# Alternating dK products with o, dQ and dV products on TensorE, and giving VectorE both gradient products in one unit of eight

## The chip, the cores and the metric

One core of a Trainium2 chip; the batches of runs fell on different chips, so each had its own runs of the kernel before beside it. The time is device microseconds (us) of one execution; lower is better. Each program ran several times.

Names: TensorE (PE in the profile, its weight loads PEld) does matrix products into PSUM, the memory that products land in, cut into banks that tiles use in turn. VectorE (DVE), ScalarE (ACT) and GpSimd (POOL) do elementwise work; taking a result out of PSUM is called an eviction. SP issues DMAs.

Tiles in the profile: `sps` scores in PSUM, `eT` their exponentials, `eN` the same transposed by DMA; `dps` the gradient product in PSUM, `cp` its copy, `dsT` the gradient of the scores, `dsx` its transpose; `oq` the PSUM bank of o and dQ, `oTs` the copy of o out of it; `qX` the queries that dK needs. Names in `R` are long-lived buffers.

## The reference, cut to what matters

The program is the forward pass and all gradients of two attention blocks. Block A, linear attention, runs first and is not touched. The change sits in block B: attention of 16 query heads over one shared key and value head, sequence 2048, head width 28.

```python
scores = jnp.einsum("bhqd,bkd->bhqk", q, k) * (Dh ** -0.5)
p = _softmax(scores, axis=-1)
o = jnp.einsum("bhqk,bkd->bhqd", p, v)
# and its gradients (jax.vjp): dV = p^T do, dS = p * (do v^T - rowsum), dQ = dS k, dK = dS^T q
```

## The kernel before

Block B is one software-pipelined loop of 512 *units* (plus a tail). Eight units make a *block*: two heads, 256 queries, all 2048 keys, 256 keys a unit. In unit `u` the kernel starts the scores of unit `u`, the gradient product for the scores of unit `w = u - 16`, and consumes older results. Two banks of PSUM (`psD`, two buffers, two tiles a unit) hold the gradient product, three hold scores.

```python
for u in range(NU + 28):
    w = u - 16
    # ... two score tiles sp, two gradient tiles dp
    rows_SD(u, sp, dp)                       # TensorE: scores of u, dP of w
    if hasS:                                 # ScalarE
        nc.scalar.activation(out=et[:, u % 2, 0, :], in_=sp[0][:, :], func=ACT.Exp, scale=scale)
    if hasD:
        nc.vector.tensor_tensor(out=dst[:, 0, :], in0=dp[0][:, :], in1=ew[:, w % 2, 0, :], op=ALU.mult)
        cp = pc_.tile([P, 512], BF16, name="cp")
        nc.scalar.activation(out=cp[:, :], in_=dp[1][:, :], func=ACT.Copy)
        nc.gpsimd.tensor_tensor(out=dst[:, 1, :], in0=cp[:, :], in1=ew[:, w % 2, 1, :], op=ALU.mult)
    if hasS:
        nc.scalar.activation(out=et[:, u % 2, 1, :], in_=sp[1][:, :], func=ACT.Exp, scale=scale)
    # ... once a block: transposes of o (unit 1) and of do (unit 6), small products
    x = u - 28                               # dK: 16 groups of 4 products a block, in units 4 to 7, 0, 1
    # ...
    v = u - 1
    y = u - 18                               # o of the unit before, dQ of the dsT two units old
    for t2 in range(2):
        # o:  vaug x eT of v        dQ:  kn x dsT[y]
    if u >= 18 and u % 8 in (2, 3):          # dV, half of it in each of two units
        # ...
    if 0 <= v < NU and v % 8 == 7:           # unit 0: VectorE takes o out of PSUM (oTs)
        nc.vector.tensor_copy(out=oTs[v // 8][:, :], in_=oq[0:64, 0:256])
    if 0 <= y < NU and y % 8 == 7:           # unit 1: ScalarE takes dQ out of PSUM
        nc.scalar.activation(out=qT_B[g][...], in_=oq[64:128, 0:256], func=ACT.Copy, scale=scale)
    # VectorE: 32x32 transposes of dsT[u - 18] into dsx, for dK
```

So `dsT`, the gradient of the scores, has two halves: VectorE makes one straight from PSUM. The other is copied by ScalarE (`cp`) and multiplied by GpSimd, because GpSimd cannot read PSUM (the Trainium skill, "Trainium Kernel Development and Optimization", Key Constraints).

Of the kernel before, what the change touches and what calls it, by code (L numbers as in the profile page):

```python
# [8 lines left out]
ACT = mybir.ActivationFunctionType  # L9
ALU = mybir.AluOpType  # L10
AX = mybir.AxisListType
BF16 = mybir.dt.bfloat16
# [5 lines left out]
P = 128  # L18
# [6 lines left out]
def kernel(  # L25
# [21 lines left out]
    nc = tc.nc  # L47
# [518 lines left out]
    NB = 64  # L566
    NU = NB * 8
# [3 lines left out]
    with ExitStack() as cs_:  # L571
# [8 lines left out]
        pc_ = cs_.enter_context(tc.tile_pool(name="ccp", bufs=3, side="right"))  # L580
# [7 lines left out]
        eT, eN, dsT, dsx, qX, onat, don, doT, rl, oTs, prod = ({} for _ in range(11))  # L588

        def mmt(out, lhsT, rhs, pos, start, stop):  # L590
            nc.tensor.matmul(out, lhsT=lhsT, rhs=rhs, start=start, stop=stop, tile_position=pos,  # L591
                             skip_group_check=True)

        def blk(b):
            qc, pair = divmod(b, 8)
            return qc, pair, pair // 2, pair % 2
# [91 lines left out]
        with tc.manual_schedule():  # L688
            for u in range(NU + 28):
                w = u - 16  # L690
# [12 lines left out]
                dp = [psD.tile([P, 512], F32, name="dps") for _ in range(2)] if hasD else None  # L703
# [7 lines left out]
                if hasD:  # L711
                    dst = pd_.tile([P, 2, 512], BF16, name="dsT")
                    dsT[w] = dst
                    ew = eT[w // 2]
                    nc.vector.tensor_tensor(out=dst[:, 0, :], in0=dp[0][:, :], in1=ew[:, w % 2, 0, :], op=ALU.mult)  # L715
                    cp = pc_.tile([P, 512], BF16, name="cp")
                    nc.scalar.activation(out=cp[:, :], in_=dp[1][:, :], func=ACT.Copy)  # L717
                    nc.gpsimd.tensor_tensor(out=dst[:, 1, :], in0=cp[:, :], in1=ew[:, w % 2, 1, :], op=ALU.mult)  # L718
                if hasS:
                    nc.scalar.activation(out=et[:, u % 2, 1, :], in_=sp[1][:, :], func=ACT.Exp, scale=scale)  # L720
                    if u % 2 == 1:
# [5 lines left out]
                if e >= 0 and e % 8 == 0 and e // 8 < NB:  # L727
                    b = e // 8
# [6 lines left out]
                    if pair == 0:  # L735
# [9 lines left out]
                                            op=ALU.mult)  # L745
# [7 lines left out]
                if e >= 0 and e % 8 == 0 and e // 8 < NB:  # L753
                    b = e // 8
# [3 lines left out]
                        out=prod[b][:],  # L758
                        in0=do_nat[:, 2 * qc:2 * qc + 2, pair * 64:pair * 64 + 64].rearrange(
                            "p q (h c) -> p q h c", c=32),  # L760
                        in1=onat[qc][:, :, pair * 64:pair * 64 + 64].rearrange("p q (h c) -> p q h c", c=32),
                        op=ALU.mult)
                e = u - 12
                if e >= 0 and e % 8 == 0 and e // 8 < NB:
                    b = e // 8
# [4 lines left out]
                if e >= 0 and e % 8 == 0 and e // 8 < NB:  # L770
                    b = e // 8
# [7 lines left out]
                    doT[b] = pw_.tile([P, 256], BF16, name="doT")  # L779
                    nc.vector.tensor_copy(out=doT[b][r:r + 64, :], in_=tp2[r:r + 64, 0:256])  # L780

                x = u - 28
                if 0 <= x and x // 8 < NB and x % 8 < 6:
                    b = x // 8
                    qc, pair, g, hp = blk(b)
                    m0 = 3 * (x % 8) - max(0, x % 8 - 4)
                    for m in range(m0, m0 + (3 if x % 8 < 4 else 2)):
                        h, B, s = m // 8, (m // 2) % 4, m % 2
                        for a in range(4):
                            rhs = dsx[b][32 * a:32 * a + 32, :, h, :, :].rearrange(  # L790
                                "p u t (b i s) -> p u t b i s", b=4, s=2)[:, :, :, B, :, s]
                            mmt(dk_acc[32 * a:32 * a + 32, :],
                                qX[qc][32 * a:32 * a + 32, B, s, pair * 64 + 32 * h:pair * 64 + 32 * h + 32],
                                rhs, (32 * a, 32 * a), b == 0 and m == 0, b == NB - 1 and m == 15)

                v = u - 1
                y = u - 18
                for t2 in range(2):
                    if 0 <= v < NU:
                        b, tp = divmod(v, 8)  # L800
                        t = 2 * tp + t2
                        for h in range(2):
                            mmt(oq[32 * h:32 * h + 32, 0:256], vaug[:, t, :],
                                eT[v // 2][:, v % 2, h, t2 * 256:(t2 + 1) * 256], (0, 32 * h), t == 0, t == 15)
                    if 0 <= y < NU:
                        b, tp = divmod(y, 8)
                        t = 2 * tp + t2
                        for h in range(2):
                            mmt(oq[64 + 32 * h:96 + 32 * h, 0:256], kn[:, t, :],
                                dsT[y][:, h, t2 * 256:(t2 + 1) * 256], (0, 64 + 32 * h), t == 0, t == 15)  # L810
                if u >= 18 and u % 8 in (2, 3) and (u - 18) // 8 < NB:
                    b, h = divmod(u - 18, 8)
                    for qb in range(2):
                        for c in range(4):
                            rhs = eN[4 * b + c][:, :, :].rearrange("p (u h t q) k -> p u h t q k", u=2, h=2,
                                                                   t=2)[:, :, h, :, qb, :]
                            mmt(dv_acc[32 * c:32 * c + 32, :], don[b][:, qb, h, :], rhs, (0, 32 * c),
                                b == 0 and h + qb == 0, b == NB - 1 and h + qb == 2)
# [20 lines left out]
                if u % 64 in (16, 24) and u > 64:  # L839
                    out_proj(2 * (u // 64 - 1) + u % 64 // 8 - 2)  # L840

                if 0 <= v < NU and v % 8 == 7:
                    oTs[v // 8] = pm_.tile([64, 256], F32, name="oTs")
                    nc.vector.tensor_copy(out=oTs[v // 8][:, :], in_=oq[0:64, 0:256])  # L844
                if 0 <= y < NU and y % 8 == 7:
                    qc, pair, g, hp = blk(y // 8)
                    nc.scalar.activation(out=qT_B[g][64 * hp:64 * hp + 64, qc * 256:(qc + 1) * 256],
                                         in_=oq[64:128, 0:256], func=ACT.Copy, scale=scale)
                if 0 <= y < NU:
                    b, tp = divmod(y, 8)  # L850
                    if tp == 0:
                        dsx[b] = px_.tile([P, 8, 2, 2, 256], BF16, name="dsx")
                    nc.vector.transpose(  # L853
                        out=dsx[b][:, tp, :, :, :].rearrange("p h t c -> p (h t c)").bitcast(F32),
                        in_=dsT[y][:, :, :].rearrange("p h c -> p (h c)").bitcast(F32))
# [11 lines left out]
        for c in range(4):  # L867
            nc.vector.tensor_copy(out=dkvT[32:64, c * 512:(c + 1) * 512], in_=dv_acc[32 * c:32 * c + 32, :])
            nc.scalar.activation(out=dkvT[0:32, :].rearrange("p (t a i) -> p t a i", a=4, i=32)[:, :, c, :],
                                 in_=dk_acc[32 * c:32 * c + 32, :].rearrange("p (t i) -> p t i", i=32), func=ACT.Copy,  # L870
# [15 lines left out]
        for c in range(4):  # L886
            r = DC_ROWS[c]
            ps = gen(0)
            for st in range(NS):
# [3 lines left out]
                                 func=ACT.Copy)  # L893
# [44 lines left out]
```

## Time and profile before

| | before |
|---|---|
| median time | 1176 us (1173 to 1179) |
| units 16 to 511 of the loop | about 280 to 1090 us |
| a block with no output projection in it | 12.78 us |
| first exponential to first exponential, usual unit | 1.46 us |
| ScalarE start to start, 128x512 from PSUM | 0.49 us (duration 0.60) |
| GpSimd multiply, 128x512 | 1.15 us |

The table of stretches for the kernel before, 400 us in mid-loop. Columns: stretch, its length, then busy time and number of instructions of PE, PEld, DVE, ACT and POOL, the TensorE clock that was granted (1 is full), the DMA share (summed time of the packets over 16 engines, so it can pass 1), GB/s.

```profile
500.00:900.00 400.00, 383.22 (x6550) 142.05 (x6550) 357.16 (x655) 384.82 (x771) 310.71 (x339) 1.00 1.10 182
```

ScalarE is busy 96% and TensorE 96% of it, VectorE 89%, GpSimd 78%. TensorE's figure does not tell how near it is to its limit (the Trainium skill, "Perfetto Trace Analysis", section "Identifying the Most-Contended Engine", says so because matmuls are pipelined; E6 below comes back to it).

The timeline of ScalarE before, one block; columns are start, length, engine, line, operation, output and input, count and, in brackets, the idle time before. L710 is the first exponential of a unit, L847 the dQ eviction. The first line is unit 7 of the block ahead; then come units 0 to 7.

```profile
725.43 0.60 ACT L710 ACTIVATE eT<-sps 128x512 bf16<-128x512 f32 x1 [0.24 <-PE dps L591]
...
726.94 0.60 ACT L710 ACTIVATE eT<-sps 128x512 bf16<-128x512 f32 x1
...
728.39 0.61 ACT L710 ACTIVATE eT<-sps 128x512 bf16<-128x512 f32 x1
...
730.01 0.38 ACT L847 ACTIVATE R_63<-oq 64x256 bf16<-64x256 f32 x1
730.42 0.60 ACT L710 ACTIVATE eT<-sps 128x512 bf16<-128x512 f32 x1
...
731.88 0.61 ACT L710 ACTIVATE eT<-sps 128x512 bf16<-128x512 f32 x1
...
733.40 0.60 ACT L710 ACTIVATE eT<-sps 128x512 bf16<-128x512 f32 x1
...
734.85 0.61 ACT L710 ACTIVATE eT<-sps 128x512 bf16<-128x512 f32 x1
...
736.40 0.60 ACT L710 ACTIVATE eT<-sps 128x512 bf16<-128x512 f32 x1
...
738.21 0.60 ACT L710 ACTIVATE eT<-sps 128x512 bf16<-128x512 f32 x1 [0.24 <-PE dps L591]
```

Read the starts of L710: 1.45 to 1.55 us apart where ScalarE just runs through three evictions. The Trainium skill, page "ScalarE: Activation LUTs", section "What ACT_TABLE_LOAD costs", says that back-to-back ACTIVATEs overlap by about 93 ns; this trace comes near it (0.60 us long, 0.49 us apart, so 0.11 us). Only two units are longer: unit 1 with the eviction (2.03) and unit 6 (1.81). I use the distance from an odd unit to the next odd unit below, because the change works in pairs: 2.96, 3.49, 2.97 and 3.36 us into units 1, 3, 5 and 7.

The waits of the loop before (from 260 to 1090 us): engine, line, what it waited for, total us, times, longest.

```profile
POOL dsT L718 <- ACT cp L717: 155.1, 310, 7.7
...
ACT eT L710 <- PE dps L591: 28.3, 79, 2.9
```

GpSimd waits for ScalarE's copies (155 us; it has time to spare), and ScalarE's first exponential seldom waits for products (28 us). Nobody is seen waiting long for GpSimd. The group of the dQ matmuls on the page before says it too; its columns are line, engine, operation, tile names, shapes, count, then busy us and mean ns, then idle us just before and the part put down to one releaser:

```profile
L591 PE MATMUL oq<-dsT,R_65 128*32 128x256 bf16 x2048 | 203.1, 278 | 1.1 <-POOL dsT L718 0.9
```

The dQ matmuls stood 1.1 us in the whole run, 0.9 of it for GpSimd's multiply.

### The profile page before, as it was taken

The numbers are of one execution on the slowest core, as the hardware profiler recorded it, in microseconds if no ns is written. First come the engines' busy times: TensorE is split into PE (matmuls) and PEld (weight loads), VectorE is DVE, ScalarE is ACT, GpSimd is POOL, SyncE is SP. The second block draws the span as 40 slices with busy tenths as digits, with TensorE's granted clock in tenths as the row PEclk, the third lists the DMA queues.
The fourth block names the chain that finished last, engine by engine and source line by source line (L and its number), as shares of the span: only waits on it lengthen the run. The fifth ranks groups of instructions, "written<-read, shape, count | busy, mean of one in ns | idle before, by whom it ended". The sixth has DMA issues, their size and how long they took to land. (4 is left out here: it accounts for less than half of the span.)

```text
span 1172.0 us, 38434 instructions
## 1 busy us (share of the span) xinstructions
PE 1099.7 (94%) x15388; PEld 444.6 (38%) x15388; DVE 885.5 (76%) x1669; ACT 900.9 (77%) x1788; POOL 699.4 (60%) x835
## 2 busy tenths in 40 slices
PE   7999997988989999999999999999999999999998
PEld 4555543333333333333333333333333333333344
DVE  7886400336889898888889888988999899888922
ACT  3453112357989999999999999999999999999511
POOL 9000150003777777777778777877787778777900
PEclk9999998989999999999999999999999999999999
DMA  9779897059999999999999999999999999999962
GB/s 259 126 130 184 160 188 177 20 125 198 180 179 190 188 164 187 190 184 175 189 188 160 199 188 186 162 198 188 152 195 182 189 170 199 184 168 163 240 147 75
DMA packets 684435, 202.91 MB, mean 173 GB/s; under 512 B 651232, under 2 KB 679392, under 8 KB 684256
## 3 DMA queue, kind: packets, MB, share of 16 engines
q1 hardware_dynamic: 673664, 190.26, 94.8%
q10 hardware_dynamic: 9312, 6.65, 2.1%
q0 software_dynamic: 1280, 3.55, 1.1%
q8 instruction: 120, 1.97, 0.7%
q14 instruction: 59, 0.48, 0.1%
HBM read 22.83 MB, written 15.03 MB: 32 GB/s over the span
## 5 line engine op out<-in xcount | busy, mean ns | idle before, releaser
L718 POOL TENSOR_TENSOR dsT<-cp,eT 128x512 bf16<-128x512 bf16 x512 | 590.3, 1153 | 193.2 <-ACT cp L717 156.2
L715 DVE TENSOR_TENSOR dsT<-dps,eT 128x512 bf16<-128x512 f32 x512 | 347.8, 679 | 58.3 <-PE dps L591 37.6
L853 DVE STREAM_TRANSPOSE dsx<-dsT 128x512 f32<-128x512 f32 x512 | 357.8, 699 | 1.3 <-POOL dsT L718 0.3
L710 ACT ACTIVATE eT<-sps 128x512 bf16<-128x512 f32 x512 | 307.3, 600 | 42.2 <-PE dps L591 28.3
L591 PEld LDWEIGHTS <-R_65 32*128 32x128 bf16 (+1 forms) x8192 | 171.5, 92 | 403.3 <-issue 356.1
L717 ACT ACTIVATE cp<-dps 128x512 bf16<-128x512 f32 x512 | 305.1, 596 | 12.0 <-PE dps L591 11.1
L720 ACT ACTIVATE eT<-sps 128x512 bf16<-128x512 f32 x512 | 311.6, 609 | 0.0
L591 PE MATMUL dk_acc<-dsx,qX 32*32 32x512 bf16 x4096 | 290.4, 377 | 0.0
L591 PE MATMUL dps<-doT,R_65 32*128 32x256 bf16 x2048 | 253.9, 271 | 7.7 <-DVE R_64 L824 1.1
L591 PE MATMUL sps<-R_63,R_65 32*128 32x256 bf16 x2048 | 242.9, 276 | 5.9 <-ACT eT L710 2.0
L591 PE MATMUL oq<-eT,R_65 128*32 128x256 bf16 x2048 | 213.8, 278 | 2.5 <-issue 0.3
L591 PE MATMUL oq<-dsT,R_65 128*32 128x256 bf16 x2048 | 203.1, 278 | 1.1 <-POOL dsT L718 0.9
L591 PEld LDWEIGHTS <-qX 32*32 32x32 bf16 x4096 | 69.4, 89 | 94.1 <-issue 54.1
L591 PE MATMUL dv_acc<-eN,don 128*32 128x512 bf16 x1024 | 86.9, 382 | 2.5 <-DMA eN<-eT 2.5
L521 DVE TENSOR_TENSOR osb<-R_65 32x512 bf16<-32x512 bf16 x4 | 1.7, 413 | 74.2 <-ACT R_65 L518 74.2
L380 POOL MEMSET ga<- 64x448 bf16 x2 | 0.9, 468 | 90.8 <-PE agen L337 71.3
L553 POOL MEMSET R_65<- 128x16 bf16 x1 | 0.2, 172 | 70.8 <-DVE R_65 L552 70.8
L748 POOL TENSOR_TENSOR don<-R_64,rl 128x128 bf16<-128x128 bf16 x64 | 25.8, 403 | 21.4 <-DVE rl L740 21.4
L844 DVE COPY oTs<-oq 64x256 f32<-64x256 f32 x64 | 26.5, 414 | 15.1 <-PE oq L591 14.4
L731 PE MATMUL sps<-identF,oTs 64*128 64x64 f32 x128 | 21.3, 247 | 17.0 <-DVE oTs L844 10.6
L591 PEld LDWEIGHTS <-don 128*32 128x32 bf16 x1024 | 34.7, 97 | 4.0 <-issue 3.9
L79 PEld LDWEIGHTS <-R_64 128*128 128x128 bf16 x256 | 23.9, 100 | 28.0 <-issue 10.3
(216 smaller groups left out, 961.2 us busy)
## 6 DMA issues: line engine op xcount, KB each, us to landing
qX<-qn_d SPq DMA_DIRECT2D x128, 64.0 KB
out_dram<-osb ACTq DMA_DIRECT2D x44, 112.0 KB
eN<-eT SPq DMA_TRANSPOSE x256
qn_d<-dsx SPq DMA_DIRECT2D x1, 2048.0 KB
on_d<-onat SPq DMA_DIRECT2D x8, 256.0 KB
xa<-in_A_x_dram SPq DMA_DIRECT2D x8, 224.0 KB
ga<-in_grad_out_dram SPq DMA_DIRECT2D x4, 448.0 KB
xa<-in_grad_out_dram POOLq DMA_DIRECT2D x4, 448.0 KB, 4.7
```

Of the source, the lines that this page charges most:

```text
L79: nc.tensor.matmul(out_ap, lhsT=lhsT, rhs=rhs, start=start, stop=stop, tile_position=(0, 0))
L521: nc.vector.tensor_tensor(out=sq[0:32, :], in0=kT[0:32, qc * 512:(qc + 1) * 512], in1=kT[0:32, qc * 512:(qc + 1) * 512], op=ALU.mult)
L591: nc.tensor.matmul(out, lhsT=lhsT, rhs=rhs, start=start, stop=stop, tile_position=pos, skip_group_check=True)
L710: nc.scalar.activation(out=et[:, u % 2, 0, :], in_=sp[0][:, :], func=ACT.Exp, scale=scale)
L715: nc.vector.tensor_tensor(out=dst[:, 0, :], in0=dp[0][:, :], in1=ew[:, w % 2, 0, :], op=ALU.mult)
L717: nc.scalar.activation(out=cp[:, :], in_=dp[1][:, :], func=ACT.Copy)
L718: nc.gpsimd.tensor_tensor(out=dst[:, 1, :], in0=cp[:, :], in1=ew[:, w % 2, 1, :], op=ALU.mult)
L720: nc.scalar.activation(out=et[:, u % 2, 1, :], in_=sp[1][:, :], func=ACT.Exp, scale=scale)
L731: nc.tensor.transpose(onp[:, qb, :, :].rearrange("p h c -> p (h c)"), oTs[b][0:64, qb * P:(qb + 1) * P], identF[0:64, 0:64], tile_position ...
L748: nc.gpsimd.tensor_tensor(out=dn[:], in0=dnv, in1=r_[:].to_broadcast([P, 2, 2, 32]), op=ALU.mult)
L844: nc.vector.tensor_copy(out=oTs[v // 8][:, :], in_=oq[0:64, 0:256])
L853: nc.vector.transpose(out=dsx[b][:, tp, :, :, :].rearrange("p h t c -> p (h t c)").bitcast(F32), in_=dsT[y][:, :, :].rearrange("p h c -> p ...
```

## The change

Its intent: TensorE goes through fewer kinds of work per unit. Before, nearly every unit had scores, dK, then o and dQ. Now odd units have scores and dK (four groups of four at once), even units have scores and a double portion of o and dQ, with dV in two of them. And in unit 2 of a block VectorE makes both halves of dsT, which relieves ScalarE of one `cp` and GpSimd of one multiply.

```diff
-                    cp = pc_.tile([P, 512], BF16, name="cp")
-                    nc.scalar.activation(out=cp[:, :], in_=dp[1][:, :], func=ACT.Copy)
-                    nc.gpsimd.tensor_tensor(out=dst[:, 1, :], in0=cp[:, :], in1=ew[:, w % 2, 1, :], op=ALU.mult)
+                    if u % 8 == 2:
+                        nc.vector.tensor_tensor(out=dst[:, 1, :], in0=dp[1][:, :], in1=ew[:, w % 2, 1, :], op=ALU.mult)
+                    else:
+                        # cp and the GpSimd multiply as before
...
-                x = u - 28
-                if 0 <= x and x // 8 < NB and x % 8 < 6:
+                x = u - 27
+                if 0 <= x and x // 8 < NB and x % 2 == 0:
...
-                v = u - 1
-                y = u - 18
-                for t2 in range(2):
+                v, y = u - 1, u - 17
+                for d in range(4 if u % 2 == 0 else 0):
+                    t2 = d % 2
+                    v_, y_ = v - 1 + d // 2, y - 1 + d // 2
...                  # o of v_, dQ of dsT[y_]
-                if u >= 18 and u % 8 in (2, 3) and (u - 18) // 8 < NB:
+                if u >= 18 and u % 8 in (2, 4) and (u - 18) // 8 < NB:
...
-                if 0 <= v < NU and v % 8 == 7:          # oTs
+                if u % 2 == 0 and 0 <= v < NU and v % 8 == 7:
-                if 0 <= y < NU and y % 8 == 7:          # dQ eviction: was unit 1, now unit 0
+                if u % 2 == 0 and 0 <= y < NU and y % 8 == 7:
```

Note `y`: in an even unit dQ now reads `dsT[u-18]` and `dsT[u-17]`. The second was made in the unit just before.

More of the change, by code (lines that the diff above doesn't have):

```diff
@@ L715 @@
                     nc.vector.tensor_tensor(out=dst[:, 0, :], in0=dp[0][:, :], in1=ew[:, w % 2, 0, :], op=ALU.mult)
-                    cp = pc_.tile([P, 512], BF16, name="cp")
-                    nc.scalar.activation(out=cp[:, :], in_=dp[1][:, :], func=ACT.Copy)
-                    nc.gpsimd.tensor_tensor(out=dst[:, 1, :], in0=cp[:, :], in1=ew[:, w % 2, 1, :], op=ALU.mult)
+                    if u % 8 == 2:
+                        nc.vector.tensor_tensor(out=dst[:, 1, :], in0=dp[1][:, :], in1=ew[:, w % 2, 1, :], op=ALU.mult)
+                    else:
+                        cp = pc_.tile([P, 512], BF16, name="cp")
+                        nc.scalar.activation(out=cp[:, :], in_=dp[1][:, :], func=ACT.Copy)
+                        nc.gpsimd.tensor_tensor(out=dst[:, 1, :], in0=cp[:, :], in1=ew[:, w % 2, 1, :], op=ALU.mult)
                 if hasS:
@@ L780 @@
                     nc.vector.tensor_copy(out=doT[b][r:r + 64, :], in_=tp2[r:r + 64, 0:256])
-                x = u - 28
-                if 0 <= x and x // 8 < NB and x % 8 < 6:
+                x = u - 27
+                if 0 <= x and x // 8 < NB and x % 2 == 0:
                     b = x // 8
                     qc, pair, g, hp = blk(b)
-                    m0 = 3 * (x % 8) - max(0, x % 8 - 4)
-                    for m in range(m0, m0 + (3 if x % 8 < 4 else 2)):
+                    for m in range(4 * (x % 8 // 2), 4 * (x % 8 // 2) + 4):
                         h, B, s = m // 8, (m // 2) % 4, m % 2
@@ L794 @@
                                 rhs, (32 * a, 32 * a), b == 0 and m == 0, b == NB - 1 and m == 15)
-                v = u - 1
-                y = u - 18
-                for t2 in range(2):
-                    if 0 <= v < NU:
-                        b, tp = divmod(v, 8)
-                        t = 2 * tp + t2
+                v, y = u - 1, u - 17
+                for d in range(4 if u % 2 == 0 else 0):
+                    t2 = d % 2
+                    v_, y_ = v - 1 + d // 2, y - 1 + d // 2
+                    if 0 <= v_ < NU:
+                        t = 2 * (v_ % 8) + t2
                         for h in range(2):
                             mmt(oq[32 * h:32 * h + 32, 0:256], vaug[:, t, :],
-                                eT[v // 2][:, v % 2, h, t2 * 256:(t2 + 1) * 256], (0, 32 * h), t == 0, t == 15)
-                    if 0 <= y < NU:
-                        b, tp = divmod(y, 8)
-                        t = 2 * tp + t2
+                                eT[v_ // 2][:, v_ % 2, h, t2 * 256:(t2 + 1) * 256], (0, 32 * h), t == 0, t == 15)
+                    if 0 <= y_ < NU:
+                        t = 2 * (y_ % 8) + t2
                         for h in range(2):
                             mmt(oq[64 + 32 * h:96 + 32 * h, 0:256], kn[:, t, :],
-                                dsT[y][:, h, t2 * 256:(t2 + 1) * 256], (0, 64 + 32 * h), t == 0, t == 15)
-                if u >= 18 and u % 8 in (2, 3) and (u - 18) // 8 < NB:
-                    b, h = divmod(u - 18, 8)
+                                dsT[y_][:, h, t2 * 256:(t2 + 1) * 256], (0, 64 + 32 * h), t == 0, t == 15)
+                if u >= 18 and u % 8 in (2, 4) and (u - 18) // 8 < NB:
+                    b, h = (u - 18) // 8, (u - 18) % 8 // 2
                     for qb in range(2):
@@ L848 @@
                                          in_=oq[64:128, 0:256], func=ACT.Copy, scale=scale)
+                y = u - 18
                 if 0 <= y < NU:
```

## The prediction

> **What bounds the kernel now.** The loop of 512 units fills about 270 to 1095 us. In the table of stretches, ScalarE is busy 96 us of every 100 in mid-loop, TensorE (modelled) 96, VectorE 89, GpSimd 78. In the timeline, ScalarE starts its three evictions of a unit (two exponentials, one copy "cp") every 0.49 us, 1.46 us a unit. Eight units (a block) plus the 0.41 us dQ eviction need 12.13 us; the block from 725.43 to 738.21 takes 12.78 us, and the mean with output projections is 13.1 us. So ScalarE, in a tight loop with TensorE, sets the pace: the next unit's products wait for cp to free its bank (two dps buffers), and the first exponential follows 0.3 us after.
>
> **What the change does.**
> 1. TensorE segments now cost their streaming plus about 0.12 us per switch: score/gradient products 0.33, o with dQ 0.33, twelve dK products 0.76, eight 0.54. Alternating takes one switch out per unit, about 0.9 us a block. The Trainium skill ("TensorEngine Tiling (Array Packing)", Key Properties) says that changing the tiling mode drains TensorE; the 0.12 us agrees. But TensorE is not alone in setting the pace, so most of this becomes slack.
> 2. In one unit of eight, cp (0.49 us of ScalarE) and a GpSimd multiply (1.15) become a second VectorE multiply (0.61). Floors become ScalarE 11.64, VectorE about 11.6 us a block. But the second gradient bank is then freed only after two VectorE multiplies, 1.3 us or more after the products, so the next unit's exponential starts about 1.7 to 1.95 us after this one's: no gain there.
> 3. The new cost: dQ read a dsT two units old; now the odd unit's dsT is read in the very next (even) unit. A GpSimd multiply ends 2.31 us after its unit's first exponential starts (725.43 to 727.74), which is 0.85 us after the next unit's. TensorE runs its matmuls in order, so it stands there (today nobody waits for that multiply), then still has 0.21 us of o and dQ, in two even units of four 0.43 us of dV, and 0.43 us until the next exponential can start. From odd unit to odd unit: 2.31+0.05+0.21+0.1+0.43 = 3.1 us, with dV 3.55, against 2.92 for ScalarE alone.
>
> **Sum.** Pairs before (timeline from 725.43): 2.96+3.49+2.97+3.36 = 12.78. After: pair into unit 1: 3.33 (ScalarE with the dQ eviction); into 3: 3.55 to 3.8 (dV, VectorE's two products); into 5: 3.55 (dV); into 7: 3.1 to 3.3. That is 13.5 to 13.9, so +0.7 to +1.1 us a block, 64 blocks, +45 to +70 us, less a little for output projections and TensorE slack at the ends. I predict **1228 us**, 80% range 1188 to 1258. Chances: faster by over 2% 0.15, within 2% 0.13, slower 0.72.
>
> **What would show it.** TensorE in even units waiting for the GpSimd multiply of dsT (new line in the waits, some 0.3 to 0.7 us, about 200 times); ScalarE busy share in mid-loop down from 96% to near 87%, its first exponential waiting for products; longest intervals where dV follows; switching saved in the timeline (four segments per two units instead of six), turned into waits. Unit 2 of a block longer than 1.46 us in spite of only two evictions on ScalarE. DMA, clock and the part before the loop unchanged.
>
> **What would make it wrong.** If TensorE's switches cost more than 0.12 us under real stalls, the removed ones would be on the critical path, and up to 1.1 us a block (6%) could be won, as ScalarE's floor falls. If the wait for GpSimd is shorter than the timeline suggests, or dV's work fits into it, the result falls to within 2%. If VectorE, at 11.6 of some 12 us, jams after the unit with both products, it is slower than I say.

## The result, and the profile after

1249.4 us median (1243.5 to 1250.7, four runs) against 1176.1. All outputs are right. The ratio is 1.0615, with a 95% interval of 1.0568 to 1.0662: 6% slower. (Here and below a ratio is the mean time of one kernel's runs over that of the other's of the same rounds, so it is not quite the ratio of the medians.) Executions over 1.5% slower than the fastest of the same kernel are left out of the means.

The same stretch of the table after:

```profile
500.00:900.00 400.00, 349.29 (x5978) 137.43 (x5980) 343.94 (x625) 344.09 (x674) 252.19 (x281) 1.00 0.96 164
```

Every engine is less busy: ScalarE 96% to 86%, GpSimd 78% to 63%, DMA share and GB/s too. Nothing is overloaded now, so the engines are waiting on each other. The waits of the loop after, 260 to 1150 us:

```profile
POOL dsT L721 <- ACT cp L720: 328.7, 428, 7.5
ACT eT L710 <- PE dps L591: 82.6, 124, 1.6
PE oq L591 <- POOL dsT L721: 69.8, 180, 0.4
...
ACT R L849 <- DVE oTs L846: 33.0, 61, 1.6
```

The third of these is new: dQ's matmuls stand 70 us, 180 times, for GpSimd's multiply. Some of that shows up again in the second: ScalarE's first exponential stood 28 us for gradient products before and stands 83 now. The fourth is new too; E5 is about it. The group of the dQ matmuls on the page after, for the one before:

```profile
L591 PE MATMUL oq<-dsT,R 128*32 128x256 bf16 x2048 | 226.0, 277 | 76.7 <-POOL dsT L721 74.6
```

From 1.1 us to 76.7 us. The chain that ended last, by engine and by line, on the page after:

```profile
PE 37%; POOL 30%; issue 13%; ACT 10%; DVE 6%; DMA 2%; SPq 1%; POOLq 0%; ACTq 0%; DVEq 0%
POOL dsT L721 29%; PE agen L79 9%; PE dk_acc L591 8%; ACT cp L720 5%; PE oq L591 5%; PE sps L79 4%; PE sps L591 3%; PE aacc L79 3%; PE dv_acc L591 2%; ACT eT L723 2%; DVE oTs L846 2%; PE dps L79 2%; PE sps L734 1%; DVE dsT L715 1%; POOL don L771 1%
```

The multiply on GpSimd is 29% of the whole chain. (Before, the page's chain ended after 5% of the span, so it says nothing about the loop there.)

The mechanism in one pair of units, from the timeline after of all engines; unit 3 starts at 708.40 and unit 5 at 711.94.

```profile
708.40 0.60 ACT L710 ACTIVATE eT<-sps 128x512 bf16<-128x512 f32 x1 [0.83 <-PE dps L591]
...
708.89 0.59 ACT L720 ACTIVATE cp<-dps 128x512 bf16<-128x512 f32 x1
...
709.56 1.15 POOL L721 TENSOR_TENSOR dsT<-cp,eT 128x512 bf16<-128x512 bf16 x1 [1.63 <-ACT cp L720]
...
710.08 0.27 PE L591 MATMUL oq<-dsT,R 128*32 128x256 bf16 x1
...
710.77 0.27 PE L591 MATMUL oq<-dsT,R 128*32 128x256 bf16 x1 [0.42 <-POOL dsT L721]
...
710.77 0.29 PE L591 MATMUL oq<-eT,R 128*32 128x256 bf16 x2
...
710.89 0.69 PE L591 MATMUL dv_acc<-eN,don 128*32 128x512 bf16 x8
...
711.51 0.28 PE L591 MATMUL sps<-R,R 32*128 32x256 bf16 x2
...
711.94 0.60 ACT L710 ACTIVATE eT<-sps 128x512 bf16<-128x512 f32 x1 [0.45 <-PE dps L591]
```

ScalarE copies the half (708.89), GpSimd multiplies it from 709.56 to 710.71, 2.31 us after the unit's first exponential. TensorE has done the scores of unit 4 and the dQ products that it could, and from 710.35 stands 0.42 us. At 710.77 it goes on; dV (710.89) and the next scores (711.51) come behind, in order, and ScalarE, idle for 0.45 us, starts unit 5 at 711.94. The skill says that matmuls start and complete in program order ("PSUM — Partial Sum Buffer", section "Engine vs sequencer instructions"); this trace agrees: dV and the scores, which need nothing from GpSimd, start only behind the matmul that does.

ScalarE's starts in the block after (L849 is the dQ eviction; unit 7, then 0 to 7):

```profile
701.16 0.60 ACT L710 ACTIVATE eT<-sps 128x512 bf16<-128x512 f32 x1
...
702.67 0.60 ACT L710 ACTIVATE eT<-sps 128x512 bf16<-128x512 f32 x1
...
704.46 0.38 ACT L849 ACTIVATE R<-oq 64x256 bf16<-64x256 f32 x1 [0.22 <-DVE oTs L846]
704.87 0.60 ACT L710 ACTIVATE eT<-sps 128x512 bf16<-128x512 f32 x1
...
706.49 0.60 ACT L710 ACTIVATE eT<-sps 128x512 bf16<-128x512 f32 x1
...
708.40 0.60 ACT L710 ACTIVATE eT<-sps 128x512 bf16<-128x512 f32 x1 [0.83 <-PE dps L591]
...
709.91 0.60 ACT L710 ACTIVATE eT<-sps 128x512 bf16<-128x512 f32 x1
...
711.94 0.60 ACT L710 ACTIVATE eT<-sps 128x512 bf16<-128x512 f32 x1 [0.45 <-PE dps L591]
...
713.44 0.60 ACT L710 ACTIVATE eT<-sps 128x512 bf16<-128x512 f32 x1
...
715.04 0.60 ACT L710 ACTIVATE eT<-sps 128x512 bf16<-128x512 f32 x1
```

| pair into unit | before | predicted | after |
|---|---|---|---|
| 1 | 2.96 | 3.33 | 3.71 |
| 3 | 3.49 | 3.55 to 3.8 | 3.53 |
| 5 | 2.97 | 3.55 | 3.54 |
| 7 | 3.36 | 3.1 to 3.3 | 3.10 |
| block | 12.78 | 13.5 to 13.9 | 13.88 |

64 blocks times 1.10 us is 70 us; the medians differ by 73. Blocks with an output projection, two of eight, lost more: 13.74 us before, 15.27 after, and there too the longer time is in the pair into unit 1 (3.60 before, 5.09 after).

### The profile page after: what moved, and what is told of

Its sections match the earlier page's. It is cut to its first block, busy times and chain, and to the rows that moved or that the text cites. A ratio compares the mean times of both kernels' runs of the same rounds, so it can differ in the third digit from the quotient of the medians.

```text
span 1241.8 us, 38192 instructions
## 1 busy us (share of the span) xinstructions
PE 1094.1 (88%) x15379; PEld 462.1 (37%) x15388; DVE 926.1 (75%) x1733; ACT 885.5 (71%) x1724; POOL 628.5 (51%) x771
## 3 DMA queue, kind: packets, MB, share of 16 engines
q0 software_dynamic: 1280, 3.55, 1.0%
## 4 chain that ended last, share of the span: by engine, by line
PE 37%; POOL 30%; issue 13%; ACT 10%; DVE 6%; DMA 2%; SPq 1%; POOLq 0%; ACTq 0%; DVEq 0%
POOL dsT L721 29%; PE agen L79 9%; PE dk_acc L591 8%; ACT cp L720 5%; PE oq L591 5%; PE sps L79 4%; PE sps L591 3%; PE aacc L79 3%; PE dv_acc L591 2%; ACT eT L723 2%; DVE oTs L846 2%; PE dps L79 2%; PE sps L734 1%; DVE dsT L715 1%; POOL don L771 1%
## 5 line engine op out<-in xcount | busy, mean ns | idle before, releaser
L721 POOL TENSOR_TENSOR dsT<-cp,eT 128x512 bf16<-128x512 bf16 x448 | 517.0, 1154 | 338.3 <-ACT cp L720 333.6
L715 DVE TENSOR_TENSOR dsT<-dps,eT 128x512 bf16<-128x512 f32 x512 | 349.6, 683 | 70.8 <-PE dps L591 39.5
L591 PEld LDWEIGHTS <-R 32*128 32x128 bf16 (+1 forms) x8192 | 180.0, 93 | 441.1 <-issue 412.8
L723 ACT ACTIVATE eT<-sps 128x512 bf16<-128x512 f32 x512 | 308.8, 603 | 0.0
L591 PE MATMUL oq<-dsT,R 128*32 128x256 bf16 x2048 | 226.0, 277 | 76.7 <-POOL dsT L721 74.6
L720 ACT ACTIVATE cp<-dps 128x512 bf16<-128x512 f32 x448 | 265.3, 592 | 15.1 <-PE dps L591 12.5
L591 PE MATMUL sps<-R,R 32*128 32x256 bf16 x2048 | 247.8, 277 | 8.5 <-ACT eT L710 4.1
L591 PE MATMUL dps<-doT,R 32*128 32x256 bf16 x2048 | 243.8, 274 | 1.5 <-DVE R L826 1.1
L591 PE MATMUL oq<-eT,R 128*32 128x256 bf16 x2048 | 202.2, 280 | 0.0
L849 ACT ACTIVATE R<-oq 64x256 bf16<-64x256 f32 x64 | 24.3, 379 | 36.3 <-DVE oTs L846 34.1
L79 PEld LDWEIGHTS <-R 128*128 128x128 bf16 (+1 forms) x416 | 34.1, 99 | 35.4 <-issue 11.1
L717 DVE TENSOR_TENSOR dsT<-dps,eT 128x512 bf16<-128x512 f32 x64 | 43.6, 681 | 0.0
```

The costliest lines, as they stand in the source:

```text
L79: nc.tensor.matmul(out_ap, lhsT=lhsT, rhs=rhs, start=start, stop=stop, tile_position=(0, 0))
L591: nc.tensor.matmul(out, lhsT=lhsT, rhs=rhs, start=start, stop=stop, tile_position=pos, skip_group_check=True)
L717: nc.vector.tensor_tensor(out=dst[:, 1, :], in0=dp[1][:, :], in1=ew[:, w % 2, 1, :], op=ALU.mult)
L849: nc.scalar.activation(out=qT_B[g][64 * hp:64 * hp + 64, qc * 256:(qc + 1) * 256], in_=oq[64:128, 0:256], func=ACT.Copy, scale=scale)
```

## The experiments

The theories. **A**: TensorE stands, in order, for the GpSimd multiply of the unit just before, and what follows it (dV, the next scores) starts late. **B**: VectorE's unit with two multiplies is the main cost. **C**: the longer, uninterrupted dK work starves ScalarE. **D** came later: VectorE's unit pays where the dQ eviction falls into the same unit. The table collects the distances between odd units in a block with no output projection, read from each timeline as above; "ratio" is to the kernel before.

| | into 1 | into 3 | into 5 | into 7 | block | median us | ratio (95%) |
|---|---|---|---|---|---|---|---|
| before | 2.96 | 3.49 | 2.97 | 3.36 | 12.78 | 1176 | |
| after | 3.71 | 3.53 | 3.54 | 3.10 | 13.88 | 1249.4 | 1.0615 (1.0568 to 1.0662) |
| E1 before + VectorE's unit | 2.97 | 3.74 | 2.97 | 3.35 | 13.03 | 1194.4 | 1.0161 (1.0128 to 1.0194) |
| E2 after - VectorE's unit | 3.70 | 3.53 | 3.53 | 3.11 | 13.87 | 1246.7 | 1.0602 (1.0569 to 1.0635) |
| E3 after, dQ one pair later | 2.98 | 3.75 | 2.96 | 2.97 | 12.66 | 1167.6 | 0.9929 (0.9898 to 0.9961) |
| E4 after, VectorE's unit 3 | 3.71 | 3.54 | 3.24 | 3.11 | 13.60 | 1229.5 | 1.0457 (1.0429 to 1.0485) |
| E5 after, dQ eviction in unit 1 | 3.10 | 3.94 | 3.53 | 3.11 | 13.68 | 1235.2 | 1.0492 (1.0449 to 1.0534) |
| E6 = E3 - VectorE's unit | 2.98 | 4.02 | 2.97 | 2.97 | 12.94 | 1182.6 | 1.0049 (1.0014 to 1.0085) |
| E7 after, dV ahead of dQ | 3.70 | 3.35 | 3.11 | 3.10 | 13.26 | 1208.8 | 1.0276 (1.0239 to 1.0313) |
| E8 = E6, o's transposes in unit 2 | 2.98 | 3.53 | 2.96 | 2.97 | 12.44 | 1165.6 | 0.9927 (0.9865 to 0.9989) |
| E9 = E8 + VectorE's unit | 2.97 | 3.32 | 3.03 | 2.98 | 12.30 | 1162.2 | 0.9880 (0.9854 to 0.9905) |
| E10 before, o's transposes in unit 2 | 2.97 | 3.47 | 2.97 | 3.36 | 12.77 | 1179.3 | 1.0047 (1.0008 to 1.0086) |
| E11 before + VectorE's unit 1 | 2.96 | 3.73 | 2.97 | 3.36 | 13.02 | 1193.4 | 1.0150 (1.0121 to 1.0178) |
| E12 = E9, 11 eN buffers | | | | | | 1162.6 | 0.9897 (0.9871 to 0.9923) |

### E1 and E2: each part alone

E1 adds the first hunk of the change to the kernel before. E2 takes it out of the kernel after:

```diff
-                    if u % 8 == 2:
+                    if False:
```

> The kernel before with VectorE's unit alone. Theory A (TensorE standing for the GpSimd multiply of the unit just before is the main cost): this part alone costs little, because the second gradient bank comes free about 1.3 us after the products instead of 1.1, so unit 2 takes about 1.7 us instead of 1.46: +0.1 to +0.25 us a block, 1180 to 1192 us. Theory B (VectorE's unit is the main cost, by jamming VectorE): most of the +73 us shows up here, over 1220 us. If VectorE's unit pays on its own through ScalarE's lower floor: below 1165 us.

> The kernel after with VectorE's unit undone. Theory A: the waits for GpSimd stay, and the pair of units into unit 3 is bound by GpSimd and dV at 3.55 us either way: 1240 to 1258 us. Theory B: most of the loss is gone, 1170 to 1200 us.

E1 lost 1.6%, a little over the range given (1194 for 1180 to 1192). Unit 2 took 1.72 us in a plain block, as estimated, for 1.46 (the pair into unit 3: 3.74 for 3.49), and its waits (260 to 1090 us) show what held it, the release of a gradient bank by VectorE's second multiply (L717):

```profile
PE dps L591 <- DVE dsT L717: 19.4, 59, 0.3
```

In a block with an output projection, two of eight, it took 2.05 us, which the estimate left out. E2 is as slow as the kernel after. So the alternation alone makes the loss, and B falls. The two parts do not add: 1.6% alone, nothing on top of the alternation, where TensorE is late in unit 2 anyway.

### E3: dQ one pair later

```diff
-        pd_ = cs_.enter_context(tc.tile_pool(name="cdsT", bufs=4, side="right"))
+        pd_ = cs_.enter_context(tc.tile_pool(name="cdsT", bufs=5, side="right"))
-                v, y = u - 1, u - 17
+                v, y = u - 1, u - 19
```

(also eN buffers 11 to 10 for room, and one load of the tail a unit later).

> The kernel after with dQ one pair later (it reads units u-20 and u-19 instead of u-18 and u-17; a fifth dsT buffer, one eN buffer fewer to make room; the dQ eviction so moves from unit 0 to unit 2 of a block). No dQ matmul can then stand for GpSimd. Theory A: the waits of TensorE for GpSimd vanish (now 70 us), the block falls from 13.88 us to 12.0 to 12.9 us, 1140 to 1185 us. Theory B, or a theory C that the long uninterrupted dK run (16 matmuls) starves ScalarE: it stays above 1225 us.

The order of work on TensorE stays alternating, the dK run stays as long, VectorE's unit stays; what changes is the age of what dQ reads, and with it the place of the dQ eviction, which goes from unit 0 to unit 2. 1167.6 us: 82 us less than after, and 0.7% below before. Moving the eviction alone gave 14 us (E5), so most of the 82 is the age; E4 and E7 below act on the same wait without moving the eviction. In the waits of E3's loop no matmul stands for GpSimd any more, and ScalarE's first exponential waits for gradient products about as long as before the change (28 us; another 29.6 us, in 61 short gaps, have no releaser in the view):

```profile
POOL dsT L721 <- ACT cp L720: 229.2, 326, 7.5
...
ACT eT L710 <- PE dps L591: 25.7, 65, 2.4
```

A holds, C falls: with the same bursts the pairs into 5 and 7 take 2.96 and 2.97, near ScalarE's own pace (2 x 1.46 = 2.92).

### E7: dV ahead of dQ

E7 moves the dV products, unchanged, ahead of the o and dQ loop in the kernel after. GpSimd's multiply is ready no sooner; only what TensorE does ahead of the wait, and so what stands behind it, changes.

> The kernel after with the dV products ahead of o and dQ in units 2 and 4, the work and its amount unchanged. Theory A (TensorE stands in order at the dQ matmul with dV behind it): dV now fills the wait, the pair into unit 5 falls from 3.54 to about 3.1 us and the pair into unit 3 to 3.1 to 3.4: minus 35 to 55 us, 1195 to 1215 us. A theory that TensorE's amount of work or the burst of dK is what binds: within 8 us of 1249.

1208.8 us, and the pair into unit 5 falls from 3.54 to 3.11, into unit 3 from 3.53 to 3.35, as A said. This is the cleanest test that the wait costs what stands *behind* it: 40 us for an exchange of two pieces of code. In its waits (260 to 1080 us) the same line has shrunk to:

```profile
PE oq L591 <- POOL dsT L721: 23.9, 57, 0.4
```

### E4: VectorE's unit moved to unit 3

```diff
-                    if u % 8 == 2:
+                    if u % 8 == 3:
```

> The kernel after with VectorE's unit moved from 2 to 3 of a block. Theory A: the dsT of unit 3, which unit 4 reads, is then ready 1.3 us after its unit's start instead of 2.3, so the pair into unit 5 falls from 3.54 to about 3.15 us and the others stay: minus 20 to 26 us, 1222 to 1232 us. Theory B: VectorE does the same work, so the time stays within 8 us of 1249.

1229.5: minus 20 us, the pair into unit 5 at 3.24, the others as they were. VectorE does the same work in both kernels; in unit 3 it makes the dsT that the next unit reads, in unit 2 it makes one that is read two units later. In the kernel after, VectorE's unit had been put where it could not help.

### E5: the second wait

The pair into unit 1 was 0.38 us longer than predicted. The timeline of ScalarE after shows the eviction idle for 0.22 us behind VectorE's copy of o; both take their rows from one bank (`oq`), and both now fall in unit 0. E5 emits the eviction at the end of unit 1, as before the change.

```diff
-                if u % 2 == 0 and 0 <= y < NU and y % 8 == 7:
+                if u % 2 == 1 and 0 <= u - 18 < NU and (u - 18) % 8 == 7:
+                    y = u - 18
```

> The kernel after with the dQ eviction on ScalarE emitted at the end of unit 1 of a block, as before the change, instead of unit 0, where it stands behind VectorE's oTs copy. Theory A plus this second wait: the pair into unit 1, 3.71 us, falls to 3.1 to 3.3 us, the other pairs stay bound by GpSimd and dV: minus 24 to 38 us, 1211 to 1226 us. If the second wait is hidden behind the one for GpSimd: within 8 us of 1249.

Half a miss: 1235.2, minus 14. The pair into unit 1 did fall, from 3.71 to 3.10. But the pair into unit 3 rose from 3.53 to 3.94, all of it from unit 1 to unit 2 (2.01 us, 1.62 after): the eviction, 0.41 us of ScalarE, now comes there. From unit 2 to 3 it stays at 1.93 (1.91). I had expected the wait for GpSimd to cover the eviction; it covers nothing of it.

Whether that wait is needed is open. The skill ("PSUM — Partial Sum Buffer", "PSUM bank collisions raise a hardware error") says that different 32-partition quadrants of one bank can be accessed at the same time, and the copies take rows 0 to 63 and 64 to 127. No run here took the wait away; E3 and later move the eviction to unit 2.

### E6, E8 and E9: what the alternation is worth without the wait

E6 is E3 with VectorE's unit off. E8 is E6 with the transposes of o one unit later:

```diff
-                e = u - 9
+                e = u - 10
-                if u % 64 == 1 and u > 1:
+                if u % 64 == 2 and u > 2:
```

E9 is E8 with VectorE's unit back on.

> e3 (dQ one pair later) without VectorE's unit: the alternation alone with no wait for GpSimd. Unit 2 there took 2.0 us, of which VectorE's two multiplies are the end; ScalarE with the dQ eviction needs 1.87. Theory A with unit 2 bound by VectorE: minus 8 to 20 us against e3, 1148 to 1160 us. If VectorE's unit pays once TensorE has slack: above 1168.

> A try to beat the kernel before: e6 with the transposes of o one unit later (unit 2 instead of 1), so that TensorE does not stand for the oTs copy ahead of dK. If that stand is on the path: 5 to 25 us below e6. If ScalarE or VectorE is the bound there, within 4 us of e6.

> A try to beat both kernels: e8 with VectorE's unit 2 back. In e6 and e8 unit 2 carries the dQ eviction, so ScalarE needs 1.87 us there and took 2.0; with VectorE's unit it needs 1.39 and VectorE's two multiplies allow about 1.7. Theory D (VectorE's unit pays where the dQ eviction falls in the same unit): minus 0.25 to 0.35 us a block against e8, 1142 to 1152 us. If e3's gain over e6 had another cause: within 5 us of e8's 1166.

E6 is a miss, and a useful one: 1182.6, 15 us *slower* than E3. In E6 unit 2 has three evictions and the dQ eviction on ScalarE, and takes 2.00 us; in E3 VectorE's unit leaves two and the eviction, and it takes 1.73. There VectorE's unit pays.

E6 also says what the alternation brings in all once nobody stands for GpSimd: nothing (1.0049). But that nothing is a gain and a loss. The pair into unit 7 falls from 3.36 to 2.97: before the change TensorE stood for nobody in unit 6, but had the transposes of do, twelve dK products and o and dQ to do ahead of the next scores, and the unit took 1.81 us; without dK in it, it takes 1.46. TensorE in that unit of the kernel before (first exponentials at 736.40 and 738.21):

```profile
736.49 0.27 PE L776 MATMUL sps<-identB,don 128*64 128x128 bf16 x2
736.70 0.83 PE L591 MATMUL dk_acc<-dsx,qX 32*32 32x512 bf16 x12
737.45 0.28 PE L591 MATMUL oq<-eT,R_65 128*32 128x256 bf16 x2
...
737.79 0.28 PE L591 MATMUL sps<-R_63,R_65 32*128 32x256 bf16 x2
```

So TensorE did set the pace before, in one unit of eight. Against that, the pair into unit 3 rises from 3.49 to 4.02, because the dQ eviction now makes unit 2 long (2.00 for 1.46) while unit 1, which had it before, stays at 2.03. In the table of stretches TensorE is busy 95% in E6 and 96% before: the average shows none of this.

```profile
500.00:900.00 400.00, 381.29 (x6500) 165.53 (x6496) 355.68 (x649) 381.32 (x765) 310.17 (x336) 1.00 1.10 179
```

E8 gains 17 us on E6: with the transposes in unit 1, TensorE stood for them *ahead of dK*, and the 2.02 us from unit 1 to unit 2 fell to 1.53. The expectation named VectorE's copy of o as what they wait for. In E6's waits (260 to 1090 us) that is so in 14 blocks alone; in 47 they stand for ScalarE's second exponential (L723), which frees one of the three scores banks, when the copy had been done for half a microsecond (block at 832 us):

```profile
PEld sps L734 <- ACT eT L723: 18.2, 47, 0.4
...
PEld sps L734 <- DVE oTs L846: 10.0, 14, 0.7
```

E8 still has the first of these (18.5 us, 49 times), but in unit 2, which stays at 2.00 us with the dQ eviction in it.

E9 is 3 us below E8 in the median where I expected 14 to 24; the intervals of the two ratios overlap, so that step is not clear of the noise. The other branch of the expectation (within 5 us of E8) came true. Still, the plain block of E9 is the shortest of these, 12.30 us. It is 1.2% faster than before, the best ratio, and less than its block promises: 0.48 us times 64 would be 31 us, the medians differ by 14.

### E10 and E11: two controls on the kernel before

> The control for e8: the kernel before with only the transposes of o one unit later. If e8's gain over e6 (17 us) needs the alternation: within 6 us of the kernel before. If the later transposes alone give it: 1155 to 1166 us.

> The kernel before with VectorE's unit put at unit 1 of a block, where its dQ eviction falls, instead of unit 2 (e1, 1194 us). Theory D: the eviction fits into the time that ScalarE saves there, so most of e1's loss of 19 us goes: 1168 to 1185 us. If VectorE's unit costs wherever it stands in this order of work: 1190 us or more.

E10 (the same two lines as E8, on the kernel before): 1.0047, no gain, and every pair as before. E8's gain needs something else of E6. What differs is the alternation, and dQ one pair later with its eviction in unit 2; no run takes the two apart. The second may explain it: in the order before, the eviction stands in unit 1, so that ScalarE alone needs 1.46 + 0.41 = 1.87 of the 2.03 us there.

E11 (E1 with `u % 8 == 1`) refutes D as I had put it: 1193.4, as slow as E1, though the eviction falls in that unit. Its waits (260 to 1080 us) say why:

```profile
ACT R L850 <- PE oq L591: 26.6, 58, 0.9
...
PE dps L591 <- DVE dsT L717: 13.7, 58, 0.3
```

Without `cp` to do, ScalarE is early, and the eviction itself waits for dQ's last products (27 us; 5 us in the loop before). The next gradient product stands for VectorE's second multiply (L717), but it does in E3 too (13.3 us, 59 times), so that is not the difference. What differs is that VectorE has the copy of o and a transpose to finish first: in a plain block of E11 its first multiply starts 0.51 us after the unit's first exponential, in E3's unit 2 only 0.06 us after, and the units took 2.17 and 1.73 us. So D needs a condition: the offload pays where the eviction falls in the unit *and* VectorE is free at its start. That second half is read from two traces, not tested by a run of its own.

### E12: where the rest of E9 went

The waits of E9, 260 to 1090 us, with the last line much grown:

```profile
POOL dsT L721 <- ACT cp L720: 177.0, 328, 7.5
...
ACT eT L710 <- PE dps L591: 39.8, 67, 4.1
...
PE dv_acc L591 <- DMA eN<-eT: 11.4, 8, 3.2
```

The dV products stand for eN, the transposed exponentials that arrive by DMA, up to 3.2 us at a time (before: 2.5 us in all, twice). I could have starved them myself by giving up the eleventh eN buffer, so E12 gives it back and takes the room elsewhere (cwk 4 to 3, cp 3 to 2).

> e9 with the eleventh eN buffer back (room from one cwk and one cp buffer fewer). In e9 the dV products stand for the transposed copies eN arriving by DMA, 11 us in all and up to 3.2 at once, in the loop's stretches that hold a qX load. If the tenth-to-eleventh buffer is what lacks: the waits go, minus 8 to 14 us, 1148 to 1155 us. If the DMA queue itself is too slow for the shorter units: within 4 us of e9.

1162.6, no change, and the wait is still there (14.7 us). So the buffer is not it.

The blocks of the profiles say where the time is. The same queue carries the loads of qX, 16 DMAs every eight blocks. All eight of E9's waits for eN fall in the block that comes two after such a load: these seven blocks together are 17.9 us longer than E9's plain block, nearly all of it in units 2 and 3 (3.1 us in the kernel before, 24.7 in E12), and the block at the same place with no load ahead takes 12.30 like the rest. That is most of the missing gain. The packets of this queue took 96.6% of 16 engines' span in E9 (94.8% before), for the same bytes in a shorter span. So the likely reason is that the queue falls behind after a load when the units are shorter; no run here moved the loads or made the DMAs fewer, so it is argued, not shown.

## Why the prediction was right

Right in direction, size (1228, range 1188 to 1258; measured 1249, near its upper end, so the loss of 73 us is just above the sum's 45 to 70) and mechanism. Point by point:

- **Switches.** Said: 0.12 us each, one less per unit, mostly slack. In the total E6 agrees (1.0049), though not unit by unit: unit 6, where TensorE set the pace, gained 0.35 us, and the later dQ eviction cost as much and more. The skill's page "TensorEngine Tiling (Array Packing)", Key Properties, says that a change of tiling mode drains TensorE; the cost seen was 0.10 to 0.11 us.
- **VectorE's unit.** Said: no gain in its unit, and part of the 3.55 to 3.8 for the pair into unit 3. Alone it cost 1.6% (E1), more than the estimate in E1's expectation; in the kernel after it cost nothing (E2), and the pair came out at 3.53.
- **The wait for GpSimd.** Said: a multiply ends 2.31 us after its unit's start, pairs of 3.1 and 3.55 us. Measured: 2.31, 3.10 and 3.54. E3, E4 and E7 each acted on this wait in a different way, and the pairs moved as A said.
- **The signs.** Said: dQ waits for GpSimd about 200 times for 0.3 to 0.7 us; it was 180 times, 70 us, 0.39 us on average. Said: ScalarE busy near 87%; it was 86%.
- **What was missed.** The pair into unit 1: 3.33 predicted, 3.71 measured. The sum took ScalarE's own work there as the limit and left out that the dQ eviction, moved into unit 0, would stand behind VectorE's copy of o, which itself waits for the late o and dQ products. That is 0.38 us a block, 24 us over 64 blocks, about the distance from 1228 to 1249, though that is arithmetic and no test: E5 shows the pair at 3.10 without it, and also that the total gets only 14 us back. Blocks with an output projection were put at a little less loss and had more, 1.53 us for 1.10. That the plain block still fell inside 13.5 to 13.9 is partly luck: the pair into unit 3 stayed below its estimate and the pair into unit 7 at the low end of its own.

## What to carry to other kernels

Before regrouping work on an in-order engine, work out for every operand how old it is when it is read, in the new order, and compare that with the slowest path that makes it: here reading a half of `dsT` one unit after it was made, and no longer two, was behind most of a loss of 6%, and reading it one pair later, with one more buffer, brought it back. Put work that depends on nothing fresh ahead of a matmul that may wait, because the wait costs what stands behind it (40 us for moving dV up). And taking work off the busiest engine pays only where what then holds the unit (here VectorE's second multiply, which frees a bank) ends before the work taken off would have: the same offload cost 19 us (E1), did nothing (E2) or gained 15 us (E3 against E6), depending on what else stood in its unit.

## What the Trainium skill lacked or had wrong

- "TensorEngine Tiling (Array Packing)", Key Properties: says that a mode change drains TensorE but not at what cost. Here eight dK products to the next kind of work took 0.54 us, twelve 0.76 and sixteen 0.98 (kernel after), so four take 0.22, and the switch is about 0.10; o and dQ to the next scores took 0.33 us for eight products and 0.55 for sixteen (E3), so about 0.11. From eight products of o and dQ to dV, which has the same tile shape (128x32), it took 0.22: no switch cost, as the page would have it.
- "Perfetto Trace Analysis", "Identifying the Most-Contended Engine": it says to optimize the engine with the highest occupancy first. ScalarE had 96%, and one of its 25 evictions a block taken away made the program 1.6% slower (E1). An average over a block of eight units also hid that TensorE, busy 96% before and 95% in E6, set the pace in one of the eight (1.81 us for 1.46).
- "PSUM — Partial Sum Buffer": it treats collisions and their rule, but not what the number of PSUM buffers costs when it ties the engines together. Here the gradient products stood 19.4 us, 59 times, for VectorE to free one of two banks (E1: 1.72 us in unit 2 for 1.46), and the transposes of o 18.2 us, 47 times, for ScalarE to free one of three (E6).
